# Second convolution filtered in triples of outputs, first convolution's sums finished in PSUM: one change to a speech joint network on one core

## The chip, the cores and the metric

One core of a Trainium2 chip. The metric is the device time of one execution in microseconds (us). Each kernel was executed several times beside the kernel before on the same chip, and medians are quoted. Each execution also records its span (first to last instruction, about 2 us less than the time) and the mean granted clock of TensorE, as a share of full speed. An execution counts as "slow" when it is over 1.5% above the fastest of its own kernel.

## The reference, cut to what matters

```python
B, T, D, K, U = 2, 4000, 512, 5, 8                     # bf16
h = gelu(conv1d(x, w1, taps=5, pad=2))[:, ::2, :]      # 2 x 2000 x 512: every second output
f = gelu(conv1d(h, w2, taps=5, pad=2))[:, ::2, :]      # 2 x 1000 x 512
fe = f @ w_f;  ge = g @ w_g
j = tanh(fe[:, :, None, :] + ge[:, None, :, :])        # 2 x 1000 x 8 x 512
return j @ w_o
```

Both convolutions have stride 2 and five taps, so an output has three even and two odd taps. Computed directly, an output costs five products of (data) x (weights), each a 512x512 matrix product, which these kernels issue as 16 matmuls of 128x128 weights.

## The kernel before: the parts that matter

Neighbouring outputs share inputs. The kernel combines inputs and weights beforehand so that two outputs cost seven products instead of ten ("filtering": polynomials are evaluated at 0, 1, -1 and infinity, multiplied, and interpolated). The products at 0 and infinity are called *end products* here (`a0`, `b1`, `b3`, `a3`); those at 1 and -1 are `b2`, `a1`, `a2`. A *unit* is one tile of time (500 pairs of outputs) by one quarter of the 512 output channels. VectorE makes the combined inputs (`xf`, "transforms"); ScalarE copies neighbours for them (`shift`), drains one bank (`cs`) and applies GELU.

```python
def xf(src, off, dst, c0, n, which, keep=False):       # VectorE: one combined input, 4 x n elements bf16
    # ... cut
    elif which == "a2":
        tt("dve", ph(2), ph(2), ph(0), sub)

class Tile_:
    def banks(self, m):                                # four PSUM banks a unit, two sets of four
        # ... cut
        base = (count["unit"] % 2) * 4 * NT
        r = (base, base + NT, base + 2 * NT, base + 3 * NT, NT)

    def products(self, unit, order=("b2", "a1", "a2", "a0", "b1", "b3", "a3")):   # TensorE: all seven
        # ... cut
        for which in order:
            bank = home[which] // NT
            self.product(which, m, home[which], bank not in begun)

    def post(self, m, where, vec=(), scal=(), first=()):
        A, C, Dd, step = where                         # ends in A and A+step, b2+a1 in C, a2 in Dd
        # ... cut
        act(c, ps.cols(C, n), ACT.Copy, scale=0.5)     # ScalarE
        flush()                                        # GELU of the unit before
        for f in scal: f()
        for s, f in ((0, 0.5), (1, -0.5)):             # VectorE: t[s] = 0.5 C +- 0.5 Dd, in SBUF
            o = t[s, 0:n]
            pl.op("dve", lambda e, o=o, f=f: e.scalar_tensor_tensor(
                out=o.ap, in0=d.ap, scalar=f, in1=c.ap, op0=ALU.mult, op1=add), (d, c), (o,))
        for f in vec: f()                              # transforms for the next tile
        tt("dve", tv, tv, ps.pair(A, step, n), add)    # + end products, still in SBUF
        pending.append(lambda: self.gelu(m, tv))

for qi in range(1, len(tiles)):                        # tiles 1..4: conv1, 5..6: conv2
    for m in range(NK):
        # ... cut
        where = tile.products(unit)
        tile.post(m, where, vec, scal, first)
        if qi == 3:                                    # conv2's combined weights, all on GpSimd
            wsum13(w2_sb, w2_t, "pool", m * P, (m + 1) * P)
            wsum04(w2_sb, w2_t, "pool", m)
        if qi == 6 and m == 0:
            fe(0)
        if qi == 6 and m in (1, 2):                    # first row of the output stage, one unit ahead
            for k_ in {1: (0, 1), 2: (2, 3)}[m]:
                tanh(0, k_)
```

The program gives each engine one queue of instructions, and the timelines below show each engine's work in that order; semaphores are put in where one reads what another wrote. In this kernel TensorE never reads or adds to anything that VectorE made from the *same* unit. VectorE and ScalarE only empty banks, and as units take turns at two sets of four banks, they may lag while the other set fills; the waits listed for TensorE are 2.2 us, all at the start.

Of the kernel before, what the change touches and what calls it, by code (L numbers as in the profile page):

```python
# [7 lines left out]
ACT = mybir.ActivationFunctionType  # L8
# [3 lines left out]
P = 128  # L12
# [189 lines left out]
def bass_standalone__seq2seq_rnn_t_joint__speech_kernel(  # L202
# [25 lines left out]
    NP1, NP2 = T1 // 2, T2 // 2  # L228
    SEG = NP1 // 2
    XW = 528  # L230
    HOFF, HWID = 2, 504
# [6 lines left out]
    with ExitStack() as es:  # L238
# [9 lines left out]
        x_off = cur[0]  # L248
# [3 lines left out]
        w1_t = at("w1_t", [3, NK, D], BF16)  # L252
        xt = [at(f"xt{i}", [4, NK, NT], BF16) for i in range(2)]
        w2_sb = at("w2_sb", [K, NK, D], BF16)
        w2_t = at("w2_t", [2, NK, D], BF16)
# [4 lines left out]
        hT = [at(f"hT{b}", [4, NK, HWID], BF16) for b in range(B)]  # L260
        xr = [Buf(nc, f"xr{i}", [4, NK, P], BF16, h_off + 16384 + i * 4096) for i in range(2)]
        assert xr[1].end <= cur[0]
        cs = [at(f"cs{i}", [NT], FP32) for i in range(2)]
        ty = [at(f"ty{i}", [2, NT], FP32) for i in range(3)]
        ssum = at("ssum", [NK, P], FP32)
# [6 lines left out]
        seg_bytes = xs[0].bytes  # L272
        fT = [at(f"fT{b}", [NK, T2], BF16, x_off + seg_bytes + b * 8192) for b in range(B)]
        feT = [at(f"feT{b}", [NK, T2], FP32, x_off + (2 - 2 * b) * seg_bytes) for b in range(B)]
        jT = at("jT", [NK, RING], BF16, w1_off)
        ost = [at(f"ost{i}", [NT], BF16, h_off + i * 1024) for i in range(NSLOT)]
        assert jT.end <= xt[0].end - xt[0].bytes and ost[-1].end <= h_off + hT[0].bytes
# [36 lines left out]
        memset(xs[1][0, :, NT:NT + 1])  # L314
# [9 lines left out]
        def load_x(s, ph, lo, hi):  # L324

            b, half = s // 2, s % 2
            off = 12 if half else 16
            i0 = half * SEG + lo - off
            dst = xs[s % 3][ph, :, lo:hi]
            src = x[b, 4 * i0 + ph:4 * (i0 + hi - lo - 1) + ph + 1:4, :]  # L330
            pl.dma("sp", lambda e: e.dma_start_transpose(out=dst.ap, in_=src), (), (dst,))
# [83 lines left out]
        def weight(wsb, wt, which, k, m):  # L415
            sl = slice(m * P, (m + 1) * P)
            taps = {"a0": 0, "b1": 1, "b3": 3, "a3": 4}
            if which in taps:
                return wsb[taps[which], k, sl]
            if which == "a1":  # L420
                return w1_t[2, k, sl] if wsb is w1_sb else w2_sb[2, k, sl]
            return wt[{"a2": 0, "b2": 1}[which], k, sl]

        def wsum13(wsb, wt, eng, lo=0, hi=D):
            v = wt[1, :, lo:hi]
            tt(eng, v, wsb[1, :, lo:hi], wsb[3, :, lo:hi], add)
            if eng == "dve":
                act(v, v, ACT.Copy, scale=2.0)
            else:
                pl.op(eng, lambda e: e.tensor_scalar(out=v.ap, in0=v.ap, scalar1=2.0, scalar2=None, op0=ALU.mult), (v,), (v,))  # L430

        def w1sums(m, part):
# [4 lines left out]
            s = ty[0][:] if m == 2 else ty[1][m]  # L437
            s = s.map(lambda a: (a if m < 2 else a.rearrange("p s c -> p (s c)")).rearrange("p (k c) -> p k c", k=NK))
# [7 lines left out]
        def wsum04(wsb, wt, eng, m):  # L446
            sl = slice(m * P, (m + 1) * P)
            s = ssum[:]
            tt(eng, s, wsb[0, :, sl], wsb[4, :, sl], add)
            tt(eng, wt[0, :, sl], s, wsb[2, :, sl], sub)  # L450
            tt(eng, wsb[2, :, sl], s, wsb[2, :, sl], add)

        count = {"unit": 0}

        class Tile_:
            def __init__(self, layer, b, src, off, dst, c0, i0, n, keep=False):
                self.layer, self.b, self.i0, self.n, self.keep = layer, b, i0, n, keep
                self.a = (src, off, dst, c0, n)
                self.w = (w1_sb, w1_t) if layer == 1 else (w2_sb, w2_t)
# [7 lines left out]
            def pairs(self, which, m):  # L467
                return [(weight(*self.w, which, k, m), operand(*self.a, which, k, self.keep)) for k in range(NK)]

            def banks(self, m):  # L470

                if self.n <= 256:
                    base = (count["unit"] % 4) * 2 * NT
                    r = (base, base + 256, base + NT, base + NT + 256, 256)
                else:
                    base = (count["unit"] % 2) * 4 * NT
                    r = (base, base + NT, base + 2 * NT, base + 3 * NT, NT)
                count["unit"] += 1
                return r

            def product(self, which, m, o, start):
                mm(ps.cols(o, self.n), self.pairs(which, m), start, True, False)

            def open(self, m):
                A, E, C, Dd, step = self.banks(m)
                home = {"a0": A, "b1": A, "b3": E, "a3": E, "b2": C, "a1": C, "a2": Dd}
                return m, home, set(), (A, C, Dd, step)

            def products(self, unit, order=("b2", "a1", "a2", "a0", "b1", "b3", "a3")):
                m, home, begun, where = unit  # L490
                for which in order:
                    bank = home[which] // NT
                    self.product(which, m, home[which], bank not in begun)
                    begun.add(bank)
                return where

            def gelu(self, m, src):

                n = self.n
                if self.layer == 1:  # L500
                    j = HOFF + self.i0 // 2
                    o = hT[self.b][:, m, j:j + n // 2].map(
                        lambda a: a.rearrange("p (par s) c -> p s par c", s=2))
                    src = src.map(lambda a: a.rearrange("p s (c par) -> p s par c", par=2))
                else:
                    o = fT[self.b][m, 2 * self.i0:2 * (self.i0 + n)].map(
                        lambda a: a.rearrange("p (c s) -> p s c", s=2))
                act(o, src, ACT.Gelu_apprx_tanh)

            def post(self, m, where, vec=(), scal=(), first=()):  # L510
# [9 lines left out]
                for f in scal:  # L520
                    f()
                d = ps.cols(Dd, n)
                for s, f in ((0, 0.5), (1, -0.5)):
                    o = t[s, 0:n]
                    pl.op("dve", lambda e, o=o, f=f: e.scalar_tensor_tensor(  # L525
                        out=o.ap, in0=d.ap, scalar=f, in1=c.ap, op0=ALU.mult, op1=add), (d, c), (o,))
                for f in vec:
                    f()
                tv = t[:, 0:n]
                tt("dve", tv, tv, ps.pair(A, step, n), add)  # L530
                pending.append(lambda: self.gelu(m, tv))

        def flush():
            while pending:
# [4 lines left out]
        NA = 254  # L539
        LATE0 = ("a0", "b1", "b3", "b2", "a1", "a2", "a3")  # L540
        tiles = [Tile_(1, 0, xs[0], 16, xt[1], 0, 0, NA, True), Tile_(1, 0, xs[0], 16 + NA, xt[0], 0, NA, 500 - NA),
                 Tile_(1, 0, xs[1], 12, xt[1], 0, 500, 500),
                 Tile_(1, 1, xs[2], 16, xt[0], 0, 0, 500), Tile_(1, 1, xs[0], 12, xt[1], 0, 500, 500)]
        tiles += [Tile_(2, b, hT[b], HOFF, xt[b], 0, 0, NP2) for b in range(B)]
# [33 lines left out]
        wsum13(w1_sb, w1_t, "dve")  # L578
# [10 lines left out]
        for b in range(B):  # L589
            for ph in (2, 3):  # L590
                memset(hT[b][ph, :, HOFF - 1:HOFF])
            memset(hT[b][0, :, HOFF + NP2:HOFF + NP2 + 1])
# [11 lines left out]
        def post0(m, first=()):  # L604
            A = base0[m]
            t0.post(m, (A, A + NT, A + NT + 256, 256), (), (), first)
# [14 lines left out]
        tiles[2].xf("a0")  # L621


        def load_rest():
            memset(xs[0][0, :, NT:NT + 1])
# [9 lines left out]

        def ge():
            for m in range(NK):
                o = ps.cols((count["unit"] % 2) * 4 * NT + m * BU, BU)
                mm(o, [(wg_sb[k, m * P:(m + 1) * P], gT[k]) for k in range(NK)], True, True)
            act(geT[:], ps.cols((count["unit"] % 2) * 4 * NT, NK * BU), ACT.Copy)  # L640

        nbank = [0]

        def bank():
            nbank[0] += 1
            return ((nbank[0] - 1) % 8) * NT
# [23 lines left out]

        for qi in range(1, len(tiles)):
            tile = tiles[qi]
            nx = tiles[qi + 1] if qi + 1 < len(tiles) else None
            if qi == 2:
                load_rest()
            for m in range(NK):
                unit = early if qi == 2 and m == 1 else tile.open(m)
                if qi == 1 and m == 0:
                    where = tile.products(unit, LATE0)
                elif qi == 2 and m == 0:  # L680
                    tile.products(unit, LATE0[:-1])
                    early = tile.open(1)
                    tile.products(early, ("a0", "b1"))
                    where = tile.products(unit, ("a3",))
                elif qi == 2 and m == 1:
# [95 lines left out]
```

## Time and profile before

| | before |
|---|---|
| time, median (4 runs) | 278.19 us (277.84 to 278.75) |
| span of the profiled run | 276.5 us |
| TensorE (PE) busy | 271.3 us, 98% |
| VectorE (DVE) / ScalarE (ACT) / GpSimd (POOL) busy | 68% / 59% / 11% |
| TensorE waits listed | 2.2 us, all at the start |

From the profile page of the kernel before. The rows of digits are 40 equal slices of the span: the busy share of PE in tenths (9 is 90% or more), and the granted clock in tenths of full speed. The last line is the chain of waits that ended last, by engine (a q marks an engine's sequencer, "issue" time in which the profile shows no wait).

```profile
span 276.5 us, 3847 instructions
PE 271.3 (98%) x1422; PEld 136.7 (49%) x1422; DVE 188.9 (68%) x249; ACT 163.0 (59%) x194; POOL 30.9 (11%) x38
PE   8899999999999999999999999999999999999995
PEclk9999999999999999999999999999999999999999
PE 96%; DMA 2%; SPq 0%; ACT 0%; issue 0%
```

The table of TensorE's waits (what it waited for, us in total, times, longest):

```profile
PE acc L298 <- DVE zero L305: 1.2, 1, 1.2
PE acc L298 <- DMA w_sb<-in_w_dram: 1.0, 1, 1.0
```

TensorE is the bottleneck, at full clock, and waits for nobody once it runs. Its timeline in one conv1 unit and at the entry to the output stage (start us, us, engine, line, operation, out<-in, shape, count; an idle time before the group would follow in brackets):

```profile
53.66 1.85 PE L298 MATMUL acc<-xt,w_sb 128*128 128x500 bf16 x8
55.35 1.01 PE L298 MATMUL acc<-xs,w_sb 128*128 128x500 bf16 x4
...
59.56 1.85 PE L298 MATMUL acc<-xt,w_sb 128*128 128x500 bf16 x8
...
158.63 3.62 PE L298 MATMUL acc<-wo_sb,jT 128*128 128x512 bf16 x16
```

No line has brackets; from one `x8` group to the next, one unit of 28 matmuls, are 5.90 us, or 0.211 us per matmul of 500 columns. The output stage follows the last product of conv2 without a gap.

### The profile page before, as it was taken

The numbers are of one execution on the slowest core, as the hardware profiler recorded it, in microseconds if no ns is written. First come the engines' busy times: TensorE is split into PE (matmuls) and PEld (weight loads), VectorE is DVE, ScalarE is ACT, GpSimd is POOL, SyncE is SP. The second block draws the span as 40 slices with busy tenths as digits, with TensorE's granted clock in tenths as the row PEclk, the third lists the DMA queues.
The fourth block names the chain that finished last, engine by engine and source line by source line (L and its number), as shares of the span: only waits on it lengthen the run. The fifth ranks groups of instructions, "written<-read, shape, count | busy, mean of one in ns | idle before, by whom it ended". The sixth has DMA issues, their size and how long they took to land.

```text
span 276.5 us, 3847 instructions
## 1 busy us (share of the span) xinstructions
PE 271.3 (98%) x1422; PEld 136.7 (49%) x1422; DVE 188.9 (68%) x249; ACT 163.0 (59%) x194; POOL 30.9 (11%) x38
## 2 busy tenths in 40 slices
PE   8899999999999999999999999999999999999995
PEld 4798844444444444444444444444444444444442
DVE  2899997977966785775433374766766766766764
ACT  2747839357228525624256385849957957966930
POOL 1000000079995000000000000000000000000000
PEclk9999999999999999999999999999999999999999
DMA  7999999992000000000000021444444444444444
GB/s 254 285 165 234 205 194 195 293 322 64 2 0 0 2 0 0 0 2 0 0 1 2 0 76 38 154 152 152 153 154 153 152 154 153 151 150 154 147 149 142
DMA packets 54720, 31.85 MB, mean 115 GB/s; under 512 B 31647, under 2 KB 54447, under 8 KB 54703
## 3 DMA queue, kind: packets, MB, share of 16 engines
q1 hardware_dynamic: 54558, 31.55, 42.4%
q8 instruction: 11, 0.18, 0.3%
q10 hardware_dynamic: 144, 0.07, 0.1%
q14 instruction: 7, 0.05, 0.1%
HBM read 7.86 MB, written 16.38 MB: 88 GB/s over the span
## 4 chain that ended last, share of the span: by engine, by line
PE 96%; DMA 2%; SPq 0%; ACT 0%; issue 0%
PE acc L298 96%; DMA w_sb<-in_w_dram 2%; SPq L322 0%; ACT ost L291 0%
## 5 line engine op out<-in xcount | busy, mean ns | idle before, releaser
L298 PE MATMUL acc<-wo_sb,jT 128*128 128x512 bf16 (+1 forms) x504 | 108.3, 377 | 0.0
L741 DVE CAST ost<-acc 128x512 bf16<-128x512 f32 (+1 forms) x105 | 72.2, 689 | 35.6 <-PE acc L298 35.6
L298 PEld LDWEIGHTS acc<-wo_sb,jT 128*128 128x128 bf16 x504 | 49.3, 98 | 58.8
L298 PE MATMUL acc<-xt,w_sb 128*128 128x500 bf16 (+2 forms) x368 | 76.9, 347 | 0.0
L291 ACT ACTIVATE jT<-feT,geT 128x1000 bf16<-128x1000 f32 (+5 forms) x84 | 70.9, 917 | 0.0
L298 PEld LDWEIGHTS acc<-xt,w_sb 128*128 128x128 bf16 x368 | 36.0, 98 | 31.4
L525 DVE SCALAR_TENSOR_TENSOR ty<-acc,cs 128x500 f32<-128x500 f32 (+2 forms) x54 | 30.4, 605 | 23.1 <-PE acc L298 23.1
L291 ACT ACTIVATE cs<-acc 128x500 f32<-128x500 f32 (+2 forms) x27 | 14.2, 530 | 46.2 <-PE acc L298 46.2
L287 DVE TENSOR_TENSOR ty<-ty,acc 128x1000 f32<-128x1000 f32 (+2 forms) x27 | 28.6, 1058 | 13.6 <-PE acc L298 13.3
L291 ACT ACTIVATE ost<-acc 128x512 bf16<-128x512 f32 (+1 forms) x21 | 12.3, 585 | 31.5 <-PE acc L298 31.5
L298 PE MATMUL acc<-xs,w_t 128*128 128x500 bf16 (+2 forms) x140 | 30.1, 340 | 0.0
L291 ACT ACTIVATE xt<-xs 128x2000 bf16<-128x2000 bf16 (+2 forms) x14 | 21.5, 1567 | 4.7 <-DMA xs<-in_x_dram 4.7
L291 ACT ACTIVATE hT<-ty 128x1000 bf16<-128x1000 f32 (+2 forms) x19 | 18.1, 951 | 6.9 <-DVE ty L287 6.9
L298 PE MATMUL acc<-xs,w_sb 128*128 128x500 bf16 (+2 forms) x104 | 19.4, 318 | 1.0 <-DMA w_sb<-in_w_dram 1.0
L298 PEld LDWEIGHTS acc<-xs,w_t 128*128 128x128 bf16 x140 | 13.5, 97 | 11.2 <-issue 0.4
L298 PE MATMUL acc<-xt,w_t 128*128 128x500 bf16 (+2 forms) x88 | 17.2, 327 | 0.0
L287 DVE TENSOR_TENSOR xt<-xt,xs 128x2000 bf16<-128x2000 bf16 (+2 forms) x14 | 16.0, 1153 | 0.4 <-ACT xt L291 0.3
L298 PE MATMUL acc<-hT,w_t 128*128 128x500 bf16 x64 | 16.1, 374 | 0.0
L298 PE MATMUL acc<-fT,wf_sb 128*128 128x500 bf16 x64 | 13.8, 374 | 0.0
L298 PEld LDWEIGHTS acc<-xs,w_sb 128*128 128x128 bf16 x104 | 10.0, 97 | 7.2 <-DMA w_sb<-in_w_dram 1.2
L291 ACT ACTIVATE fT<-ty 128x1000 bf16<-128x1000 f32 x8 | 10.5, 1315 | 3.6 <-DVE ty L287 3.6
L298 PEld LDWEIGHTS acc<-xt,w_t 128*128 128x128 bf16 x88 | 8.6, 98 | 5.8
(42 smaller groups left out, 133.8 us busy)
## 6 DMA issues: line engine op xcount, KB each, us to landing
out_dram<-ost SPq DMA_DIRECT2D x109, 128.0 KB, 1.9
w_sb<-in_w_dram SPq DMA_DIRECT2D x10, 512.0 KB, 5.6
xr<-in_x_dram SPq DMA_DIRECT2D x2, 512.0 KB, 3.8
wg_sb<-in_w_g_dram SPq DMA_DIRECT2D x1, 512.0 KB, 9.1
wf_sb<-in_w_f_dram SPq DMA_DIRECT2D x1, 512.0 KB, 7.0
wo_sb<-in_w_o_dram SPq DMA_DIRECT2D x1, 512.0 KB, 7.8
xs<-in_x_dram SPq DMA_TRANSPOSE x16, 5.1
out_dram<-ost SPq DMA_DIRECT2D x2, 120.0 KB
```

The source lines that it names most:

```text
L287: pl.op(eng, lambda e: e.tensor_tensor(out=o.ap, in0=a.ap, in1=b.ap, op=op), (a, b), (o,))
L291: pl.op("act", lambda e: e.activation(o.ap, i.ap, func, scale=scale, bias=0.0 if bias is None else bias.ap), rd, (o,))
L298: ins = e.matmul(o.ap, lhsT=l.ap, rhs=r.ap, start=start and n == 0, stop=stop and n == len(pairs) - 1, skip_group_check=not check)
L525: pl.op("dve", lambda e, o=o, f=f: e.scalar_tensor_tensor(out=o.ap, in0=d.ap, scalar=f, in1=c.ap, op0=ALU.mult, op1=add), (d, c), (o,))
L741: pl.op("dve", lambda e, o=o, v=v: e.tensor_copy(out=o.ap, in_=v.ap), (v,), (o,))
```

## The change

The intent: TensorE is the limit, so give it fewer columns. conv2 takes outputs in *triples* (evaluation at 0, 1, -1, 2 and infinity for the even taps, 0, 1, -1 and infinity for the odd ones): nine products per three outputs instead of seven per two. And VectorE loses an addition of 1000 columns per unit: it writes the combinations of the inner products *back into PSUM*, and TensorE then puts the end products on top, accumulating, so that ScalarE takes GELU straight from PSUM.

That TensorE may add to what another engine has written was the assumption: the end products are issued without the flag that begins a new sum (`False` below).

The core of the diff (buffer addresses, the first tile and the borders are cut):

```diff
-        for s, f in ((0, 0.5), (1, -0.5)):                # into SBUF
-            o = t[s, 0:n]
-            pl.op("dve", ... scalar_tensor_tensor(out=o.ap, ...))
-        tt("dve", tv, tv, ps.pair(A, step, n), add)
+    def unit(self, m, vec=(), scal=()):                   # conv1
+        C, Dd = lo * NT, (lo + 1) * NT                    # two banks a unit
+        self.product("b2", m, C, True)
+        self.product("a1", m, C, False)
+        self.product("a2", m, Dd, True)
+        act(c, ps.cols(C, n), ACT.Copy, scale=0.5)
+        for o, f in ((C, 0.5), (Dd, -0.5)):
+            stt("dve", ps.cols(o, n), ps.cols(Dd, n), f, c)    # back into PSUM
+        finish()                                          # end products + GELU of the unit before
+        for f in list(scal) + list(vec): f()
+        def end():
+            self.product("a0", m, C, False); self.product("b1", m, C, False)
+            self.product("b3", m, Dd, False); self.product("a3", m, Dd, False)
+            self.gelu(m, ps.pair(C, NT, n))
+        ends.append(end)
 # ... cut
+class Triple:                                             # conv2, three banks a unit
+    def unit(self, m, steps=(), mid=()):
+        # five inner products t1 s1 | tm sm | t2, then:
+        act(c, P_(b1), ACT.Copy, scale=0.5)
+        stt("dve", s, P_(bm), 0.5, c)
+        stt("dve", d, P_(bm), -0.5, c)
+        stt("dve", y, P_(b2), 1.0 / 3.0, d)
+        stt("dve", P_(bm), P_(b2), 2.0 / 3.0, s)
+        stt("dve", P_(b2), P_(b2), 1.0 / 6.0, s)
+        for f in mid: f()
+        finish()
+        self.gelu(1, m, y)
+        for f in steps: f()                               # transforms of the other batch
+        # end(): t0 s0 onto b2, GELU; ti si onto bm, GELU
 # ... cut
-    wsum13(w2_sb, w2_t, "pool", ...); wsum04(w2_sb, w2_t, "pool", m)
+    def w2sums(m):                                        # a quarter of conv2's combined weights
+        t, v = ssum[0][:], ssum[1][:]
+        tt("pool", t, w(0), w(4), add)
+        tt("pool", v, t, w(2), sub)
+        act(w2_t[0, :, sl], v, ACT.Copy, scale=1.0 / 3.0)
+        stt("dve", v, w(4), 4.0, w(0))
+        stt("dve", w2_t[1, :, sl], w(2), 2.0, v)
+        tt("pool", w(2), t, w(2), add)
+        act(w(0), w(0), ACT.Copy, scale=0.5)
 # ... cut
-    if qi == 6 and m in (1, 2):                           # tanh of the first output row
+    if b == 1 and m in (2, 3):
```

The end products of unit *u* stand in TensorE's queue behind the inner products of unit *u+1*, but they need VectorE to have combined unit *u*.

## The prediction

> **What bounds the kernel.** TensorE. The page gives it 271.3 of 276.5 us busy; the chain of waits that ended last is 96% TensorE; the table of waits shows it waiting 2.2 us in all, at the start. The clock is 0.9 or more in every slice. So matmul time removed is time saved, unless TensorE now waits.
>
> **Removed.** In the timeline matmuls of 500 columns follow each other every 0.211 us, of 246 every 0.105. Interpolated, 334 columns take 0.142 us. conv2 goes from 2x4x7x4=224 matmuls (47.2 us) to 2x4x9x4=288 (40.9 us): 6.3 us less. conv1 computes 2004 columns for 2000: +0.2. Net 6.1 us, all on TensorE's path. VectorE also loses its last 1.1 us addition per conv1 unit.
>
> **What is added.** Before, VectorE only drained PSUM; eight banks let it lag several us without stopping TensorE. Now the end products (four per conv1 unit, four per conv2 triple) accumulate on sums that VectorE has written, so TensorE must wait for it. [...] The allowance is one unit: about 5.9 us for 500 columns, 5.1 for a triple, 3 for 252. I compare it with work queued ahead on VectorE/ScalarE, in the program's order, with durations from the trace (pair of 500-column combinations 1.2 us, 2000-element bf16 addition 1.1, ScalarE shift 1.8, tanh of 1000 1.02, when back to back):
>
> 1. Second tile (252 columns). VectorE is already saturated from 8 to 43 us (timeline). TensorE reaches the first end products near 27.5; the combination stands behind three old-style drains (until 27.8), a transform, another drain and a transform: done near 32.2. Stall 4.5 to 5 us.
> 2. conv2 weight sums: a GpSimd-ScalarE-VectorE-GpSimd ring per quarter, about 6.5 us against 5.9, with ScalarE's PSUM copy behind it. About 2 us in all. GpSimd sums before took 1.16 to 2.0 us.
> 3. Last conv1 tile: ScalarE doubling 3.6, then 4032-element subtraction 2.2, one more 0.8, two weight sums 2.3, ahead of the second combination. Stall about 3.5. [...]
> 4. First triples of conv2: the same doubling and subtraction for the other batch, after its last GELU: about 3.3, then 0.5.
> 5. Entry to the output stage: tanh of the first row moves from one unit ahead to directly before its matmul; two GELUs and two tanh follow the last finished triple. Stall about 3.2.
>
> Sum 16.5 to 18 us of waits against 6.1 saved.
>
> **Prediction.** 278.1 - 6.1 + 17 = 289 us (+4%), range 280 to 296. Faster by over 2%: 0.05; within 2%: 0.20; slower: 0.75.
>
> **What would show it.** TensorE busy near 266 (a pipelined matmul's own record may be longer), instructions up by 64. The table of waits, empty before, names VectorE combinations for TensorE (12 to 14 us) and the tanh for about 3. Timeline: a 4.5 us gap between 27 and 33; one of 3 to 4 near 100, one near 127; one before the first output matmul. From the first output matmul to the end, nothing changes beyond the delayed end products (2.3 us) that now fall there. Conv2 matmuls at 0.142 us pace.
>
> **What would make it wrong.** Combinations written to PSUM faster than those to SBUF; transforms shorter than scaled; GpSimd's ring faster; the first-tile transforms' data arriving later (worse). If TensorE hardly waits in 2 to 4, time lands near 281[...].

What went of the argument is why a matmul adds to VectorE's sums, a second source for the time of an addition, and a variant "near 294" under a slower subtraction; the trace of the kernel after shows that 4032-element subtraction at 2.26 us, against the 2.2 that item 3 counts. "A pipelined matmul's own record may be longer": in the kernel before, matmuls of 500 columns have records of 373 to 374 ns and follow each other every 211.

## More of the kernel before

VectorE's combinations, from the groups of instructions by shape (after the bar: busy us, mean ns; after the second bar: idle time before them and what ended it):

```profile
L525 DVE SCALAR_TENSOR_TENSOR ty<-acc,cs 128x500 f32<-128x500 f32 x40 | 25.3, 673 | 23.1 <-PE acc L298 23.1
```

## The result, and the profile after

| | before | after |
|---|---|---|
| time, median of 4 | 278.19 us | 300.50 us (298.69, 302.31, 296.15, 303.60) |
| span of the profiled run | 276.5 us | 296.7 us |
| TensorE busy | 271.3 us | 272.5 us |
| TensorE waits listed | 2.2 us | 21.2 us |
| mean granted clock, run by run | 1.0 | 0.977, 0.960, 0.983, 0.955 |

The ratio is 1.0688 (95% interval 1.0635 to 1.0741): slower. A ratio is the mean time of one kernel's fast runs over that of the other's of the same rounds, so it is not quite the ratio of the medians; here two of the four runs counted as slow. The profile is of the first run, a fast one.

The page of the kernel after, the same lines as before:

```profile
span 296.7 us, 4039 instructions
PE 272.5 (92%) x1486; PEld 143.9 (49%) x1486; DVE 185.5 (62%) x268; ACT 173.1 (58%) x220; POOL 17.9 (6%) x30
PE   7897699999977979986999959999999999999995
PEclk9999799999995999999999989999999999999999
PE 69%; DVE 12%; ACT 7%; DMA 5%; issue 5%; SPq 0%; DVEq 0%; ACTq 0%
```

There are 64 matmuls more, as predicted, but they are shorter; TensorE's work should have shrunk by six us and its busy time grew by one. Two things are new: PE has slices below 9, and the clock row has a 7, a 5 and an 8. The chain of waits leaves TensorE for 31% of the span.

TensorE's waits after:

```profile
PE acc L305 <- DVE acc L447: 10.2, 4, 4.3
PE acc L305 <- DVE xs L294: 4.0, 1, 4.0
PE acc L305 <- ACT jT L298: 3.3, 1, 3.3
PE acc L305 <- DVE zero L312: 1.2, 1, 1.2
PE acc L305 <- DMA w_sb<-in_w_dram: 1.2, 1, 1.2
PE acc L305 <- DVE ty L294: 0.7, 1, 0.7
PE acc L305 <- ACT hT L298: 0.6, 1, 0.6
```

L447 is the combination, L294 a transform or a weight sum, `jT` the tanh. The sum is 21.2 us, 19.0 more than before. On TensorE's timeline:

```profile
32.61 1.84 PE L305 MATMUL acc<-xt,w_sb 128*128 128x252 bf16 x8 [4.28 <-DVE acc L447]
...
37.06 1.02 PE L305 MATMUL acc<-xt,w_sb 128*128 128x252 bf16 x8
...
91.08 1.84 PE L305 MATMUL acc<-xs,w_t 128*128 128x498 bf16 x4 [4.01 <-DVE xs L294]
92.72 3.57 PE L305 MATMUL acc<-xt,w_sb 128*128 128x504 bf16 x8
...
109.21 1.84 PE L305 MATMUL acc<-xt,w_sb 128*128 128x498 bf16 x8 [1.98 <-DVE acc L447]
...
136.21 1.88 PE L305 MATMUL acc<-row,w_sb 128*128 128x334 bf16 x12 [3.47 <-DVE acc L447]
...
174.87 4.45 PE L305 MATMUL acc<-wo_sb,jT 128*128 128x512 bf16 x12 [3.28 <-ACT jT L298]
```

Read it twice. First the brackets, which give the idle time just before a group and what ended it: five waits of 2 to 4.3 us. Then the durations. The eight matmuls of 252 columns after the first wait took 1.84 us; the same eight at 37.06 took 1.02. Four of 498 columns after the second wait took 1.84, as much as eight of them at 109.21. The stretches after the two longest waits, by windows (us, busy time with counts of PE, PEld, DVE, ACT, POOL, then the granted clock, DMA share, GB/s):

```profile
32.60:35.60 3.00, 2.99 (x15) 2.15 (x16) 3.00 (x6) 1.35 (x2) 0.00 (x0) 0.50 1.60 192
35.60:39.00 3.40, 3.40 (x33) 2.97 (x32) 2.92 (x5) 0.99 (x3) 0.00 (x0) 1.00 0.75 110
91.00:97.00 6.00, 5.92 (x15) 2.17 (x16) 2.68 (x5) 1.73 (x3) 2.19 (x2) 0.50 0.00 0
```

TensorE is busy in all three, but for 3 us after the first wait and 6 us after the second its clock was 0.50. "Busy" hides this: a matmul at half clock is busy for nearly twice as long (1.84 against 1.02 us for the same eight).

So the span's growth of 20.2 us has three terms. The work: a unit of conv2 had 28 matmuls in 5.90 us and a triple has 36 in 5.11 (0.142 us each), so eight of each give 47.2 - 40.9 = 6.3 us less, and conv1's four extra columns cost about 0.2. Waits: 19.0 us more. Half clock: span x (1 - mean clock) = 296.7 x 0.023 = 6.8 us, of which some 0.6 fell into the waits themselves. -6.1 + 19.0 + 6.2 to 6.8 = 19.1 to 19.7.

The four runs also explain their own spread. Span times mean clock, the span that an execution would have had at full clock, is 289.9, 288.4, 289.3 and 288.1 us. The runs differ in how long the half clock lasted (5 to 14 us lost), not in the rest. I use this *clock-free span* below; it is worked out, and slightly too low where half clock fell into a wait.

Why VectorE was late, in two places. At the first wait, VectorE's timeline:

```profile
28.11 1.19 DVE L294 TENSOR_TENSOR xt<-xt,xs 128x1992 bf16<-128x1992 bf16 x1
29.22 0.74 DVE L447 SCALAR_TENSOR_TENSOR ty<-acc,cs 128x252 f32<-128x252 f32 x2
...
30.66 1.19 DVE L294 TENSOR_TENSOR xt<-xs 128x1992 bf16<-128x1992 bf16 x1
32.03 0.76 DVE L447 SCALAR_TENSOR_TENSOR acc<-acc,cs 128x252 f32<-128x252 f32 x2 [0.18 <-ACT cs L298]
```

TensorE had its inner products done at 28.3 and waited for the last line, which stood behind two transforms and the drain of another unit. This was predicted. The wait at 91.08 was not; around it, on several engines:

```profile
83.08 1.99 POOL L294 TENSOR_TENSOR ssum<-ssum,w_sb 128x512 f32<-128x512 f32 x1
...
85.10 0.63 ACT L298 ACTIVATE w_t<-ssum 128x512 bf16<-128x512 f32 x1 [3.30 <-POOL ssum L294]
86.04 0.68 DVE L447 SCALAR_TENSOR_TENSOR ssum<-w_sb 128x512 f32<-128x512 bf16 x1
...
87.96 1.28 DVE L447 SCALAR_TENSOR_TENSOR acc<-acc,cs 128x504 f32<-128x504 f32 x2 [0.52 <-ACT cs L298]
...
89.15 1.87 DVE L294 TENSOR_TENSOR xs<-xs 128x1992 bf16<-128x1992 bf16 x1
```

This is `w2sums`: GpSimd's difference, ScalarE's third of it, VectorE's next sum into the same buffer `ssum`, and back to GpSimd. It turns once in about 7 us where a conv1 unit takes 5.9. ScalarE's drain `cs` of the running unit stands in its queue behind the ring (it came at 87.29), VectorE's combination behind `cs`, and *behind the combination* the last transform (`xs`, product `a2`) of the next tile, which TensorE was by then already asking for.

### The profile page after: what moved, and what is told of

Its sections match the earlier page's. It is cut to its first block, busy times and chain, and to the rows that moved or that the text cites. A ratio compares the mean times of both kernels' runs of the same rounds, so it can differ in the third digit from the quotient of the medians.

```text
span 296.7 us, 4039 instructions
## 1 busy us (share of the span) xinstructions
PE 272.5 (92%) x1486; PEld 143.9 (49%) x1486; DVE 185.5 (62%) x268; ACT 173.1 (58%) x220; POOL 17.9 (6%) x30
## 4 chain that ended last, share of the span: by engine, by line
PE 69%; DVE 12%; ACT 7%; DMA 5%; issue 5%; SPq 0%; DVEq 0%; ACTq 0%
PE acc L305 69%; DVE xt L294 3%; DMA xs<-in_x_dram 2%; ACT row L298 2%; DVE row L294 2%; DVE acc L447 2%; DMA w_sb<-in_w_dram 2%; DVE xs L294 2%; ACT xt L298 2%; DMA xr<-in_x_dram 1%; DVE sd L447 1%; ACT cs L298 1%; DVE w_t L294 1%; ACT fT L298 1%; DVE ty L447 1%
## 5 line engine op out<-in xcount | busy, mean ns | idle before, releaser
L305 PE MATMUL acc<-xt,w_sb 128*128 128x252 bf16 (+2 forms) x240 | 49.2, 347 | 6.9 <-DVE acc L447 6.3
L305 PE MATMUL acc<-xs,w_t 128*128 128x498 bf16 (+2 forms) x140 | 31.1, 349 | 4.7 <-DVE xs L294 4.0
L298 ACT ACTIVATE hT<-acc 128x996 bf16<-128x996 f32 (+2 forms) x16 | 14.4, 898 | 34.1 <-PE acc L305 34.1
L447 DVE SCALAR_TENSOR_TENSOR acc<-acc,cs 128x498 f32<-128x498 f32 (+2 forms) x30 | 17.5, 629 | 15.9 <-PE acc L305 9.1
L305 PE MATMUL acc<-row,w_sb 128*128 128x334 bf16 x128 | 20.8, 305 | 3.9 <-DVE acc L447 3.9
L298 ACT ACTIVATE xt<-xs 128x1992 bf16<-128x1992 bf16 (+2 forms) x14 | 21.6, 1571 | 4.5 <-DMA xs<-in_x_dram 4.5
L305 PE MATMUL acc<-xs,w_sb 128*128 128x252 bf16 (+2 forms) x104 | 20.4, 330 | 1.2 <-DMA w_sb<-in_w_dram 1.2
L305 PE MATMUL acc<-xt,w_t 128*128 128x252 bf16 (+2 forms) x88 | 17.2, 328 | 0.0
L294 DVE TENSOR_TENSOR xt<-xt,xs 128x1992 bf16<-128x1992 bf16 (+2 forms) x14 | 16.6, 1197 | 0.4 <-ACT xt L298 0.4
L447 DVE SCALAR_TENSOR_TENSOR sd<-acc,cs 128x334 f32<-128x334 f32 x16 | 7.3, 500 | 13.1 <-PE acc L305 9.0
L298 ACT ACTIVATE cs<-acc 128x498 f32<-128x498 f32 (+3 forms) x27 | 13.0, 485 | 3.5 <-PE acc L305 3.4
L294 DVE TENSOR_TENSOR row<-row,hT 128x4032 bf16<-128x4032 bf16 (+1 forms) x4 | 6.2, 1552 | 13.8 <-ACT row L298 13.8
```

The lines of the kernel that those rows point to most:

```text
L294: pl.op(eng, lambda e: e.tensor_tensor(out=o.ap, in0=a.ap, in1=b.ap, op=op), (a, b), (o,))
L298: pl.op("act", lambda e: e.activation(o.ap, i.ap, func, scale=scale, bias=0.0 if bias is None else bias.ap), rd, (o,))
L305: ins = e.matmul(o.ap, lhsT=l.ap, rhs=r.ap, start=start and n == 0, stop=stop and n == len(pairs) - 1, skip_group_check=not check)
L447: pl.op(eng, lambda e: e.scalar_tensor_tensor(out=o.ap, in0=a.ap, scalar=f, in1=b.ap, op0=ALU.mult, op1=add), (a, b), (o,))
```

## The experiments

The theory: TensorE waits where VectorE's and ScalarE's queues, in program order, put the needed instruction too late; each such wait can be removed by reordering; and after a wait of several us TensorE runs at half clock for a while, which is a cost of its own. The rivals: the slow matmuls come from adding onto sums that VectorE wrote (the change's idea itself is slow); or VectorE is simply overloaded, so that a wait removed in one place comes back in the next.

Overview. Each experiment is the kernel after with one edit, except the last three. All outputs are right. Ratios are against the kernel before; "clock-free" is span x mean clock of the fast runs.

| | median us | ratio, fast runs | clock of the runs | clock-free span | wait that went |
|---|---|---|---|---|---|
| kernel after | 300.50 | 1.0688 | 0.955 to 0.983 | 289 to 290 | |
| tanh earlier | 297.00 | one fast run only | 0.965 to 0.982 | 285 | 3.28 |
| gaps filled | 293.35 | 1.0544 | 0.988 to 0.994 | 289 to 290 | filled, not removed |
| first tile reordered | 292.78 | 1.0546 | 0.971 to 0.982 | 285 to 286 | 4.28 |
| sums one unit later | 296.03 | 1.0593 | 0.954 to 0.988 | 286 to 288 | 0.64; 4.01 to 2.05 |
| odd sums earlier | 296.57 | 1.0646 | 0.965 to 0.977 | 285 to 287 | 1.98 |
| doubling on VectorE | 293.58 | 1.0540 | 0.982 | 286 | 1.98; 3.47 to 0.97 |
| ring opened | 294.18 | 1.0576 | 0.971 to 0.977 | 285 to 286 | 0.64; 4.01 to 1.32 |
| five together | 276.86 | 0.9936 | 1.0 | 274 to 275 | all but 3.5 us in all |
| seven together | 273.79 | 0.9836 | 0.999 to 1.0 | 271 to 272 | all but 0.7 |
| seven, one wait put back | 278.48 | 1.0006 | 0.994 to 1.0 | 275 | (3.28 back) |

### The tanh of the first row, one unit earlier

```diff
-                if b == 1 and m in (2, 3):
-                    for k in (2 * m - 4, 2 * m - 3):
+                if b == 1 and m in (1, 2):
+                    for k in (2 * m - 2, 2 * m - 1):
```

> One line moved: the tanh of the first output row are issued one conv2 unit earlier. Theory (waits plus clock): the 3.3 us wait of TensorE for the tanh before the first output matmul goes, and with it the 4 us of half clock that follow (1.7 us lost): about 5.0 us faster than the changed kernel, near 292 to 293 us beside its fast runs of 296 to 299; clock after the entry to the output stage 1.0. Rival (the output stage is paced by VectorE draining and would absorb the wait, or the half clock comes at random): under 1.5 us gained, half clock still there.

Measured: 297.00 us (297.02, 297.05, 292.42, 296.99). The 3.28 us wait was gone and no other moved. But only one execution was fast, so there is no ratio of fast runs: in the other three the clock was 0.965, with half clock also after the 1.98 us wait (0.53 from 109 to 112) and after the 3.46 us one (0.50 from 137.7 to 141), where the profiled run of the kernel after had full clock. The fast run's clock-free span is 285.4, against 289.9 and 289.3 for the fast runs of the kernel after: 4 us less. So the wait was worth its length, and the time as such says little, since the half clock of the remaining waits comes and goes.

### The three gaps filled with idle matmuls

```diff
+        def idle_mm(n):
+            for _ in range(n):
+                mm(ps.cols(banks[0] * NT, NT), [(zero[0:P], zero[:])], True, True)
```

Eighteen matmuls on zeros go into the gap at 28 us, 17 into that at 87, 13 before the output stage. They write a bank that is free. They change nothing of what VectorE or ScalarE do and make nothing come sooner; they only keep TensorE from idling. This tells the half clock from the rival "adding onto VectorE's sums is slow".

> The same schedule, with throw-away matmuls of zeros put into TensorE's queue where it waited 4.3, 4.0 and 3.3 us (18, 17 and 13 of them, 0.216 us each, into a PSUM bank that is free). They do no useful work. Theory: idle time itself lowers the clock afterwards; with the gaps filled the granted clock stays at 1.0 and the 16+16+12 matmuls after them run at full pace: 1.4 + 2.9 + 1.7 = 6.0 us gained, about 291 us, although the waits for VectorE and ScalarE are as long as before. It should also spread less from run to run than 296 to 304. Rival (the lower clock is a state of the chip, unrelated to the gaps): clock stays at 0.96 to 0.98, time unchanged within 1 us or longer.

Measured: 293.35 us, ratio 1.0544 (1.0513 to 1.0576), clock 0.988 to 0.994. Timeline of TensorE in the first gap, and windows after the first and second gap:

```profile
27.60 4.06 PE L305 MATMUL acc<-zero 128*128 128x512 bf16 x18
32.36 1.02 PE L305 MATMUL acc<-xt,w_sb 128*128 128x252 bf16 x8 [0.70 <-DVE acc L447]
```

```profile
32.40:36.00 3.60, 3.60 (x34) 3.26 (x35) 3.60 (x6) 1.87 (x4) 0.00 (x0) 1.00 1.02 208
89.40:95.00 5.60, 5.59 (x27) 2.65 (x28) 2.65 (x4) 2.88 (x5) 2.11 (x2) 1.00 0.00 0
```

The first products after the gap took 1.02 us instead of 1.84, and they add onto the same sums, which VectorE wrote at the same time. The clock-free span stayed at 289 to 290: the waiting is all still there, and what came back is the half clock alone. The unfilled gap of 3.46 us in this run was followed by 0.50 again, so the clock did not reach the expected 1.0, and fast runs against fast runs (1.0688 to 1.0544) the gain is 4.0 us, not the expected 6.0. So the slow matmuls belong to the idle time and not to the sums; that rival falls.

### The first tile in another order

The combinations of the second tile's units are put before the drains and transforms that stood ahead of them.

```diff
+        where0 = t1.whole(0)
         post0(1)
         post0(2, (lambda: tiles[2].shift("a0"),))
+        t1.unit(1)
         post0(3)
+        t1.unit(2)
         tiles[2].xf("a0")
-        t1.post(0, t1.whole(0), (lambda: tiles[2].shift("b1"),))
+        t1.post(0, where0)
         tiles[2].xf("a1")
+        tiles[2].xf("a2")
+        t1.unit(3, [...xf("b1")], [...shift("b1"), ...shift("a3")])
```

> In the second conv1 tile the combinations written into PSUM are issued on VectorE before the drain of that tile's first unit and before the third tile's transforms; nothing is added or removed. Theory (place in VectorE's queue makes the wait): the 4.3 us and 0.7 us waits between 24 and 33 us shrink to under 1.5 us together and the half clock at 33 to 36 us goes (1.4 us): 5 to 6.4 us faster than the changed kernel, about 291 to 292. Rival (VectorE has too much work in this stretch whatever the order, it is 90% busy or more): the wait moves to the end products of the third tile, between 33 and 45 us, and the gain is under 2 us.

Measured: 292.78 us, ratio 1.0546 (1.0493 to 1.0599), clock-free span 285.2 to 285.6. The 4.28 us wait is not in the list any more, the 0.69 us one before it is, and the others have their old lengths (4.02, 1.98, 3.46, 0.48, 3.28). Fast against fast the gain is 4.0 us, short of the 5 to 6.4 expected: it is the length of the wait alone, since the mean clock of the fast runs was no better (0.979 against 0.980). The wait did not come back elsewhere although VectorE has as much to do as before: the rival "overload" fails here.

### conv2's weight sums, the rest one unit later

```diff
             tt("pool", v, t, w(2), sub)
+        def w2rest(m):          # what follows in the ring, called one unit later
             act(w2_t[0, :, sl], v, ACT.Copy, scale=1.0 / 3.0)
```

> The ScalarE and VectorE part of each quarter of the conv2 weight sums is issued one unit later, when GpSimd has long delivered, so that ScalarE's copy of the next PSUM sums doesn't stand behind a wait for GpSimd. Theory (the ring makes the a2 transform of the last conv1 tile late): the 4.0 us wait for that transform falls to under 1 us, the 0.6 us wait for a GELU goes, the half clock at 91 to 97 us (2.9 us) goes; the wait behind the doubling and the weight sums of the last tile grows from 2.0 to about 2.6 because TensorE arrives earlier. Net 5 to 6.5 us faster, about 291. Rival (the a2 transform is simply last in its order, the ring is harmless): the 4 us wait stays over 2.5 us and the gain is under 2.

Measured: 296.03 us, ratio 1.0593 (1.0531 to 1.0655). A half miss. The GELU wait of 0.64 us went, but the `a2` wait only fell from 4.01 to 2.05 us where I had expected under 1, the 1.98 us wait stayed at 1.98 instead of growing, and fast against fast the gain was 2.6 us instead of 5 to 6.5. The ring was moved, not opened: GpSimd, ScalarE and VectorE still hand the one buffer round, and GpSimd still waited 2.5 us a turn for VectorE.

### conv2's odd weight sums earlier

```diff
                 if qi == 3 and m == 0:
+                    w2odd()
                     tail_zero(0)
-                if qi == 4 and m == 0:
-                    w2odd()
```

> The two 2048-element weight sums are issued on VectorE at the start of the fourth conv1 tile, where it stood idle for 6 us, instead of ahead of the second combination of the last tile. Theory (queue position): the 2.0 us wait near 108 us shrinks below 0.3, nothing else changes: span times clock falls from 289 to about 287.2. Rival (the doubling on ScalarE alone makes that combination late): the wait stays over 1.5 us.

Measured: 296.57 us, ratio 1.0646 (1.0614 to 1.0677). The 1.98 us wait went, the rest kept its place and length (the tanh wait read 3.51). It had been one queue: doubling on ScalarE, then the 4032-element subtraction on VectorE (2.26 us), one more (0.85), these two sums (2.35), and the combination only then. Taking 2.35 us out was enough.

### The doubling on VectorE instead of ScalarE

```diff
-                    act(r(0, n=E), z(4, -1, E), ACT.Copy, scale=2.0)
-                    act(r(slice(1, 3), n=E), z(slice(0, 4, 2), 0, E), ACT.Copy, scale=2.0)
+                    ts2(r(0, n=E), z(4, -1, E))           # VectorE tensor_scalar, times 2
+                    ts2(r(slice(1, 3), n=E), z(slice(0, 4, 2), 0, E))
```

> The doubling of the conv2 rows is taken off ScalarE (3.6 us in two instructions, twice in the kernel) and done on VectorE, which waits for it idle. Theory: [...]the 3.5 us wait near 136 us falls to 0.6 to 2, the 2.0 us wait near 108 us to 0 to 1; span times clock falls from 289 to 285 to 288. Rival (VectorE, not the doubling, is the late part): waits stay, since VectorE has more to do.

Measured: 293.58 us, ratio 1.0540 (1.0525 to 1.0554). VectorE's timeline before the triple whose wait had been 3.47 us:

```profile
122.70 1.28 DVE L451 TENSOR_SCALAR row<-hT 128x1344 bf16<-128x1344 bf16 x2 [2.88 <-ACT hT L298]
124.02 2.26 DVE L294 TENSOR_TENSOR row<-row,hT 128x4032 bf16<-128x4032 bf16 x1
```

The two doublings take 1.28 us on VectorE and took 3.65 on ScalarE, and the next instruction needs no other engine. The 3.47 us wait fell to 0.97, the 1.98 us one went with it, 0.48 stayed. Giving VectorE *more* work shortened the waits for VectorE; so they are a matter of when, not of how much.

### The ring opened

GpSimd's four sums get a buffer each and are made first, the differences follow two quarters ahead, and the rest of a quarter one unit later, so nobody waits for `ssum` in the middle of a quarter.

```diff
-            t, v = ssum[0][:], ssum[1][:]
-            tt("pool", t, w(0), w(4), add)
-            tt("pool", v, t, w(2), sub)
+            t, v = wt[m][:], ssum[m % 2][:]               # made two quarters ahead
             act(w2_t[0, :, sl], v, ACT.Copy, scale=1.0 / 3.0)
             stt("dve", v, w(4), 4.0, w(0))
             stt("dve", w2_t[1, :, sl], w(2), 2.0, v)
+            if m < 2:
+                w2diff(m + 2)
```

> GpSimd forms the four sums and the first two differences ahead, in buffers of their own, and the ScalarE and VectorE part of a quarter comes one unit later, so that none of it waits for GpSimd. Same arithmetic. After the first attempt left a 2.05 us wait with the ring still turning once in 7 us, this opens it. Theory: the wait for the a2 transform (4.0 us in the changed kernel, 2.05 in the first attempt) falls below 0.4 and that for a GELU stays away; the half clock at 91 to 97 us is gone; the wait near 108 us is 2 to 2.8. Span times clock near 284.5 to 285.5. Rival (a2 is late because it is the last transform in its tile): over 1.5 us of that wait stays.

Measured: 294.18 us, ratio 1.0576 (1.0553 to 1.0598), clock-free span 285.1 to 285.8. The GELU wait went and the `a2` wait fell from 4.01 to 1.32 us, with full clock after it (1.00 from 87.4 to 93). I had expected under 0.4: the ring accounts for 2.7 us, and the other 1.3 is that `a2` is the last transform in VectorE's queue. The version with seven edits below moves it and leaves none.

### Five edits together

The tanh, the first tile, the odd sums, the doubling and the opened ring.

> All five together: tanh one unit earlier, first-tile order, ring opened, odd weight sums early, doubling on VectorE. If the waits are the whole loss, TensorE waits only 2 to 4 us in all, no gap reaches 2 us, the clock stays at 0.99 or more and the 6.1 us saved on TensorE come through: span 271 to 274, 273 to 276 us against 278.4 before (0.98 to 0.99). If writing sums into PSUM and adding on top costs anything beyond waiting, it stays above 280.

Measured: 276.86 us (five runs, 276.24 to 277.00), ratio 0.9936 (0.9922 to 0.9949), and the clock is 1.0 in every run. Waits left from the change: 1.33 (`a2`), 0.97, 0.48 and 0.69 us. That is 0.9 us above the expected 273 to 276; the waits left are within the 2 to 4 us expected, 3.5 in all. The edits nearly add up, and with no wait over 1.4 us left there is no half clock.

### Seven edits together

The `a2` transform of the last conv1 tile one unit earlier, and the second batch's transforms one unit later:

```diff
-                    vec = (("a1",), ("a0", "b1"), ("b3", "a3"), ("a2",))[m]
+                    vec = (("a1",), ("a0", "b1"), ("b3", "a3", "a2"), ()) if qi == 3 else (...)
-                    steps = (("2d", "r", "t2", "t1"), ("next", "prev", "ti", "t0", "tm"), ("s1", "si", "sm"), ("s0",))[m]
+                    steps = (("2d", "r"), ("next", "prev", "t2", "t1", "ti", "t0"), ("tm", "s1", "si", "sm"), ("s0",))[m]
```

> The five together left waits of 1.33 us (the a2 transform of the last conv1 tile), 0.97 and 0.48 us (first triples of conv2) and 0.69 us (second conv1 tile). Here a2 is issued one unit earlier, and two row transforms of the second batch stand behind the second triple's combinations instead of before them. Theory (queue position is all there is left): the 1.33 falls under 0.4, the 0.97 and 0.48 under 0.3 each; span 275.0 to 272.3, about 274 us, 0.985 of the kernel before. Rival: VectorE is full there and the waits only move; 276 us or more.

Measured: 273.79 us (272.96 to 273.90) against 278.35, ratio 0.9836 (0.9822 to 0.9849): faster than both kernels, though under 2%. Page and TensorE's waits:

```profile
span 271.1 us, 4022 instructions
PE 265.0 (98%) x1475; PEld 142.6 (53%) x1486; DVE 186.2 (69%) x272; ACT 165.4 (61%) x216; POOL 16.2 (6%) x30
PEclk9999999999999999999999999999999999999999
```

```profile
PE acc L307 <- DVE zero L314: 1.2, 1, 1.2
PE acc L307 <- DVE ty L296: 0.7, 1, 0.7
PE acc L307 <- DMA w_sb<-in_w_dram: 0.4, 1, 0.4
```

TensorE is busy 265.0 us, 6.3 less than before, at full clock and 98% of the span again. (This trace lacks 11 of the 1486 matmul records, which leaves small gaps of 0.6 us in all, so the saving is nearer 5.7; the span fell by 5.4 us.) This is the intended saving, delivered by the same arithmetic in the same places (triples, sums in PSUM); only the order of the other engines' work differs, one small operation has changed engine, and one buffer has become four.

### One wait put back

The seven edits, with the tanh late again: one wait of 3.28 us in a kernel that otherwise has none.

> The best version with one wait put back: the tanh of the first output row stand where the change has them. One gap in an otherwise steady kernel. Theory (a gap costs its length, and then as much again as half of the slow stretch after it): span 271.1 + 3.3 to 3.7 of waiting + 1.5 to 2.3 of lost clock = 276 to 277 us, 278 to 279 measured, clock 0.98 to 0.99. If the wait alone counts: 274.5 span, 276.3 to 277 measured, clock 1.0.

Measured: 278.48 us (six runs), ratio 1.0006 (0.9984 to 1.0029). TensorE in the profiled run:

```profile
155.17 2.76 PE L307 MATMUL acc<-wo_sb,jT 128*128 128x512 bf16 x12 [3.28 <-ACT jT L300]
```

Here the wait was followed by full clock: twelve matmuls in 2.76 us, where the kernel after had needed 4.45 for the same twelve. Of the six runs, two had clock 1.0 and spans of 275.3 and 275.4 us; four had 0.994 and 276.4 to 276.8. Against the spans without the wait (271.1 to 271.9, another chip, with the medians of the kernel before 0.12 us apart) the wait alone costs about 3.7 us, and the half clock, in four runs of six, about 1.3 more.

## Why the prediction was right or wrong

**Right: the direction and the structure.** The prediction said that TensorE would no longer be free of VectorE, and named where. Its five places came with 4.28 + 0.69 us (4.5 to 5 predicted), 0.64 (ring, "about 2"), 1.98 (about 3.5), 3.47 + 0.48 (3.3, then 0.5) and 3.28 (3.2). The tanh wait is the cleanest case: removing it, alone, gave back about 4 us; putting it back, alone, cost 3.7 without half clock.

**Right: the work saved.** 6.1 us were predicted; conv2's pace of 0.142 us per 334 columns is as predicted, and with the waits gone TensorE's busy time fell by 6.3, or 5.7 with the missing records counted.

**Not so: writing to PSUM as a risk.** The prediction listed "combinations written to PSUM faster than those to SBUF" as what could spoil it. They take the same time within 1.3%, from the groups of the kernel after:

```profile
L447 DVE SCALAR_TENSOR_TENSOR acc<-acc,cs 128x498 f32<-128x498 f32 x16 | 10.1, 679 | 10.7 <-PE acc L305 5.6 <-ACT cs L298 5.1
```

That is 679 ns for 498 columns, against 673 for 500 into SBUF.

**Wrong: the size, 300.5 us where the range ended at 296.** The step that failed is the sum "16.5 to 18 us of waits against 6.1 saved", carried into "278.1 - 6.1 + 17 = 289". It prices a wait at its length. What is missing is a term for the pace of the matmuls *after* a wait: 6.8 us in the profiled run, and 5 to 14 across the four. The symptom was in the prediction's own list of signs: "TensorE busy near 266" came out as 272.5, and as 265.0 in the kernel with seven edits, which does not wait. The gaps filled with idle matmuls show that this term belongs to the idling: the waiting unchanged, most of the clock back, 4.0 us less, fast runs against fast runs. At full clock the four runs would have taken about 290 to 292 us (clock-free span and the 2 us outside it), inside the range: an estimate, but it puts the miss on this term.

**Smaller: the list of waits.** They came to 19.0 us instead of 17. The `a2` wait of 4.01 us was not foreseen: the prediction followed the ring to ScalarE's PSUM copy ("about 2 us in all") but not on to the *last* item of VectorE's queue, a transform for the next tile. On the other side items 2 and 3 were put at 5.5 us without it; with it they are 0.64 + 4.01 + 1.98 = 6.6. That the sum came so near is partly luck: one wait was missed, and items 2 and 3 were put 1.4 and 1.5 us too long.

Together, for the profiled run: 289 predicted, + 6.8 for the half clock, + 2 for the waits = 298, and 298.7 was measured.

**What decides the cases in the middle, and what is open.** Over the profiles of the kernel after and of the ten experiments, all eleven waits of 4.0 to 4.3 us were followed by half clock; eleven of fourteen between 3.28 and 3.68 us; two of seven near 2 us; none of those up to 1.33. The clock records kept in the same traces (`clock` in trace.npz, which no view prints as a list) show a pattern. Within each trace all changes of clock lie whole multiples of 3.41 us apart (in the kernel after: half clock from 32.20 to 35.61, 90.22 to 97.05 and 175.56 to 178.97 us), and each of the 24 half-clock stretches lasts 3.41 us (16 of them) or 6.83 us (8). Cut the twelve profiles (the kernel before's among them) into these intervals, from the first full-clock record to about 7 us before the end, 958 in all, and add up TensorE's idle time in each. After an interval at full clock, half clock followed in 22 of 22 cases with 2.13 us or more idle, in none with 1.92 or less, and in two of three at 1.98. After an interval at half clock, it stayed in eight of eight cases with 0.86 us or more idle and ended in all 24 with 0.72 or less. So in these traces it mattered where a wait fell on this grid as well as how long it was: 3.28 us divided 0.56 + 2.73 in the kernel after led to half clock, and 1.43 + 1.85 in the last experiment did not. It also fits the spread: the losses of the four runs, 6.8, 12.0, 5.0 and 13.6 us, are 4, 7, 3 and 8 times 1.71, half an interval. This was read from the traces afterwards; no run was made to test it, and it is a pattern of these twelve traces, no more. The 0.69 us wait in the first tile is still there in the best version.

## What to carry to other kernels

Before you move part of a result from "drained after TensorE" to "needed by TensorE", follow the queue of the engine that makes it, instruction by instruction to its last item: its busy share (62% here) does not tell when a result comes, and nearly all the waits went by order (with one small move between engines and a few more buffers), with VectorE no less busy. Price a wait of TensorE at its length plus what a half-clock stretch after it may cost (1.7 or 3.4 us each in these traces), and look for it in the clock row, not in the busy time. A change that looks bad because of its waits may still have a sound saving: put idle matmuls into the gaps to see how much is clock, remove the waits to see how much is order.

## What else the traces measured

- With five waits of 2 to 4.3 us inside the span, half clock cost 2.3% in the profiled run (6.8 of 296.7 us) and 4.5% in the slowest (clock 0.955).
- After the 4.01 us wait the clock stood at 0.50 for 6 us with TensorE busy nearly throughout (5.92 of 6.00): the first interval of that stretch still had 0.86 us of idling, and a second one at half clock followed.
- In the kernel after, twelve bf16 additions of 1992 elements ran on VectorE: the seven with GpSimd idle took 1.19 us each, the five beside sums on GpSimd 1.87 to 2.15. GpSimd's difference took 1.15 us the one time VectorE was idle and 1.99 the three times beside such additions.
- Finishing sums in PSUM made TensorE dependent on a queue that it was free of (19.0 us more waits), while VectorE's writes there took 679 ns for 498 columns against 673 for 500 into SBUF.
